# Loads of the values' matrices put into one line with those of q and k, in a top-k attention with an MLP behind it

## The chip, the cores and the metric

The kernel runs on one core of one Trainium2 chip. The metric is the device time of a run in microseconds (us). Before the change the median of three runs is 1463.46 us (1463.31 to 1465.66).

## What is computed

Per batch (8) and head (8), with 576 queries and keys of 64 elements, float32:

```python
scores = scale * np.matmul(q, k.transpose(0, 1, 3, 2))
kth = np.partition(scores, -top_k, axis=-1)[..., -top_k:-top_k + 1]   # top_k = 32
scores = np.where(scores >= kth, scores, -1000000000.0)
attn = np.exp(scores - np.max(scores, axis=-1, keepdims=True))
attn = attn / (np.sum(attn, axis=-1, keepdims=True) + 1e-09)
attn_out = np.matmul(attn, v)
x = attn_out.transpose(0, 2, 1, 3).reshape(B * S, H * D)              # 4608 x 512
h = x @ w_in                                                          # 512 x 2048
out = np.maximum(0.01 * h, h) @ w_out                                 # 2048 x 512
```

## The kernel before

**Pairs and units.** Two heads make a pair, so there are 32 pairs, four a batch. The attention is cut into 144 units, 18 a batch: a whole unit is 128 query rows of one pair, a left unit the 64 remaining rows of two pairs. In even batches the 16 whole units come first and the 2 left units last; in odd batches the left units come first. So an odd batch begins with two left units that between them touch all four of its pairs: units 18 and 19 (pairs 4 to 7), 54 and 55 (pairs 12 to 15), 90 and 91 (20 to 23), 126 and 127 (28 to 31). An even batch begins with one whole unit of each pair (36 to 39 for pairs 8 to 11).

**Steps.** The loop over s (L629 on) runs one step a unit, and an order written out by hand spreads the units in flight over the engines; each engine runs its own instructions in that order. In step s:

- VectorE picks the 32 largest scores of unit s (`top_k`, L292 to L309: eight MAX8 and six MATCH_REPLACE8 a unit), and takes the reciprocals of unit s-2 (L330);
- GpSimd masks unit s-1 (L317, L318), ScalarE takes its exponents (L321) and normalizes unit s-2 (L333);
- `transpose` (L335) turns the weights of unit s-2: ScalarE splits them into 16-bit halves (L342), SyncE writes the two halves to DRAM (L343, tile `apart`), and, once both have landed, reads them back through a transposing DMA (L347, tile `wT`). Units 14, 15, 23 and 31 are transposed on TensorE instead (L357);
- at the end of step s, from unit 14 on, TensorE multiplies the weights of two units with the values (L386 whole, L398 left, tile `vt`). Line 513, `values_at`, says when: for unit n at the end of step (n | 1) + 3, one step earlier for units 14 and 15, 22 and 23, 30 and 31. Units 54 and 55 are therefore due at the end of step 58. ScalarE copies the result to `x` (L410);
- from step 20 on, TensorE then computes the scores of units s+2 and s+3 in even steps (L228), and ScalarE copies them out (L235);
- the MLP of finished chunks of tokens (L455 and L467, with w_in and w_out) fills TensorE between these in small portions, with a budget per portion that is set so that the work is done when the next chunk is ready.

**Kept scores.** TensorE is free in the first steps, so the scores of 12 units are computed then and written to DRAM (`keep_scores`, L285). They are those of units a, a+1, a+8 and a+9 for each a of `KEPT` (L521), and come back in a fetch of 576 KB (`fetch_scores`, L290), three steps ahead of their unit.

**SyncE.** All DMAs are issued by SyncE, in its order; one that has to wait holds back those behind it. In a step the order is: halves, transposing DMA, then one of a fetch or one waiting load of q or k (L669 to L672), later an output (L477), and at the step's end what `load_more` (L567) starts. Queries and keys go into `waiting` (L162) and leave it one transfer a step. Value matrices (320 KB a pair, five buffers) do not: `load_v` (L177) issues their load at once, at the end of step last + 4, where last is the last unit of the pair that frees the buffer. At the turn to an odd batch that makes two loads at the end of each of two steps (20 and 21, 56 and 57, 92 and 93, 128 and 129, where three are left for the last); at the turn to an even batch it makes one at the end of each of four steps (36 to 39 and so on).

Of the kernel before, what the change touches and what calls it, by code (L numbers as in the profile page):

```python
# [20 lines left out]
def kernel(  # L21
# [13 lines left out]
    nc = tc.nc  # L35
    NPAIR, P, S = qT.shape
# [20 lines left out]
    LOADED, LOADED_V = 5, 5  # L57
# [102 lines left out]
    qk_of, v_of = {}, {}  # L160

    def load_qk(pi, at_once=True):  # L162
        if pi % (LOADED + 3) < LOADED:
            qt = loads.tile([P, S], F32, name="qt")
            kt = loads.tile([P, S], F32, name="kt")
        else:
            raw = raws.tile([P, WCH, 4], U16, name="raw").rearrange("p n w -> p (n w)").bitcast(F32)
            qt, kt = raw[:, 0:S], raw[:, S:2 * S]
        waiting.extend([(qt, qT[pi]), (kt, kT[pi])])
        qk_of[pi] = qt, kt  # L170
        if at_once:
            while waiting:
                nc.sync.dma_start(*waiting.pop(0))

    waiting = []

    def load_v(pi):  # L177
        v_of[pi] = loads.tile([P, NKC, 2, D], F32, name="vt", bufs=LOADED_V)
        nc.sync.dma_start(v_of[pi], vk[pi])

    class Unit:

# [71 lines left out]
    def load_early(us):  # L254

        raw = raws.tile([P, WCH, 4], U16, name="raw").rearrange("p n w -> p (n w)").bitcast(F32)
        at = 0
        for pi in sorted({u.pairs[0] for u in us}):
            kt = raw[:, at:at + S]
            nc.sync.dma_start(kt, kT[pi])  # L260
            at += S
            for u in us:
                if u.pairs[0] == pi:
                    early_of[u] = raw[:, at:at + P], kt
                    nc.sync.dma_start(early_of[u][0], qT[pi][:, u.q0:u.q0 + P])
                    at += P
# [61 lines left out]
    def reciprocals(u):  # L328
        u.rz = small.tile([P, 2], F32, name="rz")
        nc.vector.reciprocal(u.rz, u.ze)  # L330
# [175 lines left out]
    LAG = 3  # L506
# [6 lines left out]
    def values_at(n):  # L513

        if n < UNHURRIED:
            return (n | 1) + LAG + 1, MIDDLE
        return (n | 1) + LAG - ((n | 1) in HURRIED), END

    steps = units

    KEPT = (24, 40, 56)  # L521
    EARLY_SCORES = {0: 4, 1: 2, 2: 1, 3: 2, 4: 1, 5: 2}

    def unit(n):
# [26 lines left out]

    with tc.manual_schedule():
        last = {p: n for n, u in enumerate(steps) for p in u.pairs}

        to_keep = [[steps[n] for n in (a, a + 1, a + 8, a + 9)] for a in KEPT]
        early_units = {u for us in to_keep for u in us}
        to_load, to_keep = list(to_keep), [u for us in to_keep for u in us]
        assert all(len(u.pairs) == 1 for u in to_keep)

        def score_early(count):  # L560

            for _ in range(min(count, len(to_keep))):
                keep_scores(to_keep.pop(0))
                if len(to_keep) % 4 == 0 and to_load:
                    load_early(to_load.pop(0))

        def load_more(s):  # L567

            for of, load, n, lag in ((v_of, load_v, LOADED_V, LAG + 1), (qk_of, load_qk, LOADED + 3, 8)):
                if of is qk_of and to_keep:  # L570
                    while len(of) < LOADED:
                        load(len(of))
                    continue
                while len(of) < NPAIR and (len(of) < n or last[len(of) - n] + lag <= s):
                    if of is v_of or len(of) < n:
                        load(len(of))
                    else:
                        if not waiting:
                            load(len(of), at_once=False)
                        break  # L580


        for n in range(3):
            load_weights(n)
        jobs = [round_weights(*job) for job in ROUNDED] if AS_WORDS else [iter(())] * len(ROUNDED)
        for n in range(len(jobs) + 1):
            if n == len(jobs) - 1:
                first = first_scores(steps[0])
                next(first, None)
            for job in jobs[max(n - 1, 0):n + 1][::-1]:  # L590
                next(job, None)
            if n == len(jobs) - 1:
                next(first, None)
                load_v(0)
                load_v(1)
            elif n == len(jobs):
                for _ in first_scores(steps[1]):
                    pass
            if n:
                load_weights(n + 2)  # L600
            if n >= len(jobs) - 2:
                load_early(to_load.pop(0))
            if 0 <= n - len(jobs) + HP + 1 < HP:
                load_qk(n - len(jobs) + HP + 1)

        def weights_of(u):
            reciprocals(u)
            normalize(u, 0)
            normalize(u, 1)

        def values(*place):
            due = [u for n, u in enumerate(steps) if values_at(n) == place]
            if not due:
                return ()
            po = ps_sc.tile([P, 2, 512], F32, name="wide", bufs=2)
            if len(due[0].pairs) == 1:
                weigh_whole(due, po, FULL + [NKC - 1] if place[1] == MIDDLE else
                            [QUARTERS] + FULL if place[0] < HURRY else FULL + [QUARTERS])
                return [(due[0], po[:, :, 0:P])]
            for n, u in enumerate(due):  # L620
                weigh_left(u, po[:, :, n * LEFT:(n + 1) * LEFT])
            return [(u, po[:, :, n * LEFT:(n + 1) * LEFT]) for n, u in enumerate(due)]

        def keep(weighed, *place):
            for u, po in weighed:
                keep_values(u.pairs[0], po, u.b, u.q0)
            attended(*place)

        for s in range(len(steps) + LAG + 1):  # L629
            assert s < 7 or not to_keep  # L630
            cur, old, older, new = unit(s), unit(s - 1), unit(s - 2), ()
            if s % 2 == 0:
                new = [u for u in steps[s + 2:s + 4] if u]
            picks = top_k(cur) if cur else iter(())
            budget = slot_budget(s)

            def slot():
                next(picks, None)

            at_first = s < HURRY and s - 2 in HURRIED  # L640
            if at_first:
                weights_of(older)
            slot()
            if old:
                mask(old, 0)
                mask(old, 1)
            late = s < HURRY and not {s - 1, s - 2} & set(HURRIED)
            if older and not late and not at_first:
                weights_of(older)
            mlp_steps(budget)  # L650
            weighed = values(s, MIDDLE)
            at_once = s - 2 in HASTY or any(at == (s, MIDDLE) for at, _ in ready_at)
            if at_once:
                keep(weighed, s, MIDDLE)
            slot()
            if older and late:
                weights_of(older)
            if s - 2 in HASTY:
                transpose_in_haste(older)
            mlp_steps(budget)  # L660
            if old:
                exponents(old, 0)
            mlp_steps(budget)
            if older:
                keep_transposed(older) if s - 2 in HASTY else transpose(older, lambda: mlp_steps(budget))
            if not older or s - 2 in HASTY:
                mlp_steps(budget)
            if unit(s + 3) in early_units:
                fetch_scores(unit(s + 3))  # L669
            elif waiting:  # L670
                nc.sync.dma_start(*waiting.pop(0))
            slot()  # L672
            slot()
            mlp_steps(budget)
            if old:
                exponents(old, 1)
                sums(old)
            mlp_steps(budget)
            if not at_once:
                keep(weighed, s, MIDDLE)  # L680
            if new and new[0] in early_units:
                new = ()
            if new and s < HURRY:
                scores(new)
            keep(values(s, END), s, END)
            if new and s >= HURRY:
                scores(new)
            score_early(EARLY_SCORES.get(s, 0))
            budget = slot_budget(s + 1)
            mlp_steps(budget)  # L690
            load_more(s)
        mlp_steps(1e9)

# [58 lines left out]
```

## Time and profile before

| | |
|---|---|
| median of three runs | 1463.46 us |
| the profiled execution's own time | 1460.92 us |
| its span | 1458.9 us |
| granted TensorE clock over the span | 0.983 |
| TensorE, VectorE busy | 1397.0 us, 1319.8 us |
| ScalarE, GpSimd busy | 1101.0 us, 1096.4 us |
| DMA: moved, mean rate | 239.14 MB, 164 GB/s |
| SyncE: halves, transposing DMAs, loads of values | 280, 140, 32 |
| one half, one transposing DMA, one load of values, issue to landing (median) | 2.3, 4.6, 3.8 us |

A line of a timeline gives the start, the busy time, engine and line, operation, output and inputs, how many instructions were merged, and in brackets the idle time before and what ended it. PE is TensorE, PEld its weight loads, DVE VectorE, ACT ScalarE, POOL GpSimd, SPq SyncE's queue. On SPq the time is that of issuing, and the landing is told apart.

### The profile page before, as it was taken

The page shows a single profiled execution, that of the slowest core. Times are in us where ns is not written, and L with a number is a line of the kernel's source. Part 1 is how long each engine was busy: PE and PEld are TensorE (multiplying, and loading weights), DVE is VectorE, ACT ScalarE, POOL GpSimd, SP SyncE. Part 2 cuts the span into 40 slices and gives each one's busy share as a digit, 9 for nine tenths or more (in the row PEclk, how much of TensorE's full clock was granted, in tenths as well). Part 3 has the DMA queues.
Part 4 walks back from the last instruction along what each step waited for, and adds up shares of the span by engine and source line. Part 5 has one row for each costly group of instructions (what it writes and reads, how often), then busy time and mean ns, then how long its engine had stood idle before and what let it go on. Part 6 is the DMA issues. An engine that isn't in the chain of part 4 may idle for free.

```text
span 1458.9 us, 26037 instructions
## 1 busy us (share of the span) xinstructions
PE 1397.0 (96%) x8978; PEld 904.6 (62%) x8980; DVE 1319.8 (90%) x3401; ACT 1101.0 (75%) x1984; POOL 1096.4 (75%) x744
## 2 busy tenths in 40 slices
PE   7848999899989999999999999999999999999998
PEld 2324548475656666666666666666666666666674
DVE  7999999989999999999999999999999999999600
ACT  8878888577767777778787878787878787778710
POOL 3388888878887888888888888888888888788600
PEclk9968999999999999999999999999999999999999
DMA  9967544647476676667666655557555665554610
GB/s 334 338 213 228 140 119 117 185 117 185 137 192 170 179 173 161 187 167 191 169 158 165 176 145 139 166 156 177 148 161 163 171 155 130 171 138 128 154 40 14
DMA packets 394996, 239.14 MB, mean 164 GB/s; under 512 B 334576, under 2 KB 336112, under 8 KB 392944
## 3 DMA queue, kind: packets, MB, share of 16 engines
q1 hardware_dynamic: 394864, 237.48, 58.7%
q8 instruction: 70, 1.15, 0.3%
q14 instruction: 62, 0.51, 0.1%
HBM read 55.77 MB, written 99.09 MB: 106 GB/s over the span
## 4 chain that ended last, share of the span: by engine, by line
PE 74%; DVE 12%; DMA 7%; ACT 5%; issue 1%; SPq 0%; POOL 0%; DVEq 0%; ACTq 0%; POOLq 0%
PE ph L455 28%; PE pz L467 28%; PE wide L386 9%; DVE tops L304 5%; PE wide L228 4%; DVE pairs L307 4%; DMA apart<-split 3%; PE narrow L228 3%; DMA wT<-apart 3%; ACT split L342 2%; DVE pairs L299 1%; PE wide L398 1%; ACT s_sb L321 1%; ACT s_sb L333 1%; DMA raw<-in_weights_dram 1%
## 5 line engine op out<-in xcount | busy, mean ns | idle before, releaser
L317 POOL TENSOR_SCALAR pen<-s_sb,tops 128x576 f32<-128x576 f32 x288 | 637.5, 2213 | 202.0 <-DVE tops L304 130.0
L304 DVE MAX8 tops<-pairs 128x8 f32<-128x288 f32 (+1 forms) x1152 | 636.0, 591 | 0.0
L467 PE MATMUL pz<-w_out,gT 128*128 128x512 f32 x1152 | 504.7, 594 | 2.4 <-ACT scale L428 2.4
L455 PE MATMUL ph<-x,w_in 128*128 128x256 f32 x2176 | 482.6, 381 | 0.0
L307 DVE MATCH_REPLACE8 pairs<-tops,pairs 128x288 f32<-128x288 f32 (+1 forms) x864 | 460.3, 538 | 0.0
L455 PEld LDWEIGHTS ph<-x,w_in 128*128 128x128 f32 x2176 | 409.5, 190 | 77.3 <-issue 23.1
L318 POOL TENSOR_TENSOR s_sb<-s_sb,pen 128x576 f32<-128x576 f32 x288 | 406.4, 1411 | 24.1
L467 PEld LDWEIGHTS pz<-w_out,gT 128*128 128x128 f32 x1152 | 216.4, 190 | 267.0 <-issue 261.5
L342 ACT COPY split<-s_sb 128x1152 uint16<-128x1152 uint16 x280 | 309.5, 1147 | 2.3 <-DMA apart<-split 2.2
L333 ACT ACTIVATE s_sb<-s_sb,rz 128x576 f32<-128x576 f32 x288 | 207.6, 773 | 36.9 <-DVE rz L330 36.6
L321 ACT ACTIVATE s_sb<-s_sb,nbias 128x576 f32<-128x576 f32 x288 | 222.3, 772 | 5.7 <-POOL s_sb L318 5.7
L299 DVE TENSOR_TENSOR pairs<-s_sb 128x576 f32<-128x576 f32 x288 | 213.6, 780 | 9.5
L386 PE MATMUL wide<-wT,vt 128*64 128x128 f32 (+1 forms) x2560 | 160.3, 284 | 14.5 <-DMA wT<-apart 10.9
L386 PEld LDWEIGHTS wide<-wT,vt 128*64 128x64 f32 (+1 forms) x2560 | 132.4, 139 | 63.8 <-issue 41.3
L410 ACT COPY x<-wide 128x128 f32<-128x128 f32 (+1 forms) x160 | 32.2, 260 | 130.9 <-PE wide L386 114.9
L461 ACT ACTIVATE gT<-ph 128x512 f32<-128x512 f32 x136 | 80.6, 593 | 56.1 <-PE ph L455 55.8
L235 ACT COPY s_sb<-wide 128x704 f32<-128x704 f32 x130 | 98.1, 755 | 9.4 <-PE wide L228 3.6
L476 ACT COPY o_sb<-pz 128x512 f32<-128x512 f32 x36 | 21.1, 585 | 90.3 <-PE pz L467 90.3
L228 PE MATMUL wide<-kt,qt 64*64 64x352 f32 x640 | 66.3, 476 | 1.0 <-ACT s_sb L250 0.7
L235 ACT COPY s_sb<-narrow 128x448 f32<-128x448 f32 x130 | 62.9, 536 | 0.9 <-PE narrow L228 0.4
L307 DVE MATCH_VALUE_LOAD pairs<-tops,pairs 128x8 f32 x864 | 62.7, 73 | 0.0
L330 DVE RECIPROCAL rz<-ze 128x2 f32<-128x2 f32 x144 | 22.2, 154 | 39.7 <-ACT ze L326 39.3
(69 smaller groups left out, 701.8 us busy)
## 6 DMA issues: line engine op xcount, KB each, us to landing
apart<-split SPq DMA_DIRECT2D x280, 288.0 KB, 2.3
raw<-in_weights_dram SPq DMA_DIRECT2D x15, 1024.0 KB, 7.1
vt<-in_vk_dram SPq DMA_DIRECT2D x32, 320.0 KB, 3.8
out_dram<-o_sb SPq DMA_DIRECT2D x36, 256.0 KB, 3.1
kept<-gT SPq DMA_DIRECT2D x12, 576.0 KB, 3.4
s_sb<-kept SPq DMA_DIRECT2D x12, 576.0 KB, 4.8
qt<-in_qT_dram SPq DMA_DIRECT2D x20, 288.0 KB, 3.5
kt<-in_kT_dram SPq DMA_DIRECT2D x20, 288.0 KB, 3.5
```

The source lines that it names most:

```text
L228: nc.tensor.matmul(to[r0:r0 + LEFT, i, :], qt[d, q0:q0 + LEFT], kt[d, k0:k1], start=True, stop=True)
L299: nc.vector.tensor_tensor(pairs[:, :, n, :], u.both[:, :, 0:HS], u.both[:, :, HS:S], op)
L304: nc.vector.max(out=u.tops[:, i, r, :], in_=rest[i])
L307: nc.vector.match_replace(out=rest[i], in_to_replace=u.tops[:, i, r, :], in_values=rest[i], imm_value=LOWEST)
L317: nc.gpsimd.tensor_scalar(pen, u.s[i], u.tops[:, i, ROUNDS - 1, 7:8], MASKED, ALU.is_lt, ALU.mult)
L318: nc.gpsimd.tensor_tensor(u.s[i], u.s[i], pen, ALU.add)
L321: nc.scalar.activation(u.s[i], u.s[i], AF.Exp, bias=u.nbias[:, i:i + 1], scale=SCALE, accum_out=u.z[:, i:i + 1])
L333: nc.scalar.activation(u.s[i], u.s[i], AF.Copy, bias=0.0, scale=u.rz[:, i:i + 1])
L342: nc.scalar.copy(split, pairs[:, :, h])
L386: nc.tensor.matmul(po[n * D:(n + 1) * D, side, 0:P], v_of[u.pairs[0]][k, at, side, :], u.wT[k, at + side * NKC if at + 1 < NKC else at, :] ...
L455: nc.tensor.matmul(ph[:, i, 0:n], w_in[c][:, f * P:(f + 1) * P], x[c][:, 0:n], start=(c == 0), stop=(c == HP - 1),)
L467: nc.tensor.matmul(pz[0:m, 0:DMODEL], gT[:, f, r0:r0 + m], w_out[f // 4][:, f % 4, :], start=(f == 0), stop=(f == NFC - 1),)
```

## The change

A value matrix whose buffer comes free is no longer loaded at the end of the step. It goes into a line of its own, `waiting_v`, with the step in which it is first used (`due`), and the one place in the middle of a step where loads of q and k leave, after the step's transposing DMA, now serves both: values first when they are due within three steps or when nothing else waits, and a second value matrix in the same step when it is due in the next. In a step with a fetch none leaves. A matrix may enter the line as soon as the values that free its buffer have been emitted. Besides, the first group of kept units is 26, 27, 34, 35 in place of 24, 25, 32, 33.

```diff
-    def load_v(pi):
+    def load_v(pi, due=None):
         v_of[pi] = loads.tile([P, NKC, 2, D], F32, name="vt", bufs=LOADED_V)
-        nc.sync.dma_start(v_of[pi], vk[pi])
+        if due is None:
+            nc.sync.dma_start(v_of[pi], vk[pi])
+        else:
+            waiting_v.append((due, v_of[pi], vk[pi]))
+
+    def load_waiting(s):
+
+        if waiting_v and (not waiting or waiting_v[0][0] <= s + 3):
+            nc.sync.dma_start(*waiting_v.pop(0)[1:])
+            if waiting_v and waiting_v[0][0] <= s + 1:
+                nc.sync.dma_start(*waiting_v.pop(0)[1:])
+        elif waiting:
+            nc.sync.dma_start(*waiting.pop(0))
...
-    KEPT = (24, 40, 56)
+    KEPT = (26, 40, 56)
...
+        starts = {p: n for n, u in reversed(list(enumerate(steps))) for p in u.pairs}
...
-            for of, load, n, lag in ((v_of, load_v, LOADED_V, LAG + 1), (qk_of, load_qk, LOADED + 3, 8)):
...
-                while len(of) < NPAIR and (len(of) < n or last[len(of) - n] + lag <= s):
...
+            while len(v_of) < NPAIR:
+                n = len(v_of)
+                if n < LOADED_V:
+                    load_v(n)
+                elif values_at(last[n - LOADED_V])[0] <= s:
+                    load_v(n, due=values_at(starts[n])[0])
+                else:
+                    break
+            while len(qk_of) < NPAIR:
+                n = len(qk_of)
+                if n < LOADED or not to_keep and n < LOADED + 3:
+                    load_qk(n)
+                elif not to_keep and last[n - LOADED - 3] + 8 <= s and not waiting:
+                    load_qk(n, at_once=False)
+                else:
+                    break
...
             if unit(s + 3) in early_units:
                 fetch_scores(unit(s + 3))
-            elif waiting:
-                nc.sync.dma_start(*waiting.pop(0))
+            else:
+                load_waiting(s)
```

More of the change, by code (lines that the diff above doesn't have):

```diff
@@ L173, in load_qk @@
                 nc.sync.dma_start(*waiting.pop(0))
-    waiting = []
-    def load_v(pi):
+    waiting, waiting_v = [], []
+    def load_v(pi, due=None):
         v_of[pi] = loads.tile([P, NKC, 2, D], F32, name="vt", bufs=LOADED_V)
-        nc.sync.dma_start(v_of[pi], vk[pi])
+        if due is None:
[9 more added lines that the diff above has]
+            nc.sync.dma_start(*waiting.pop(0))
     class Unit:
@@ L567, in load_more @@
         def load_more(s):
-            for of, load, n, lag in ((v_of, load_v, LOADED_V, LAG + 1), (qk_of, load_qk, LOADED + 3, 8)):
[L570 to L573, printed above, removed]
-                while len(of) < NPAIR and (len(of) < n or last[len(of) - n] + lag <= s):
[L575 to L580, printed above, removed]
+            while len(v_of) < NPAIR:
[14 more added lines that the diff above has]
+                    break
         for n in range(3):
```

## Prediction

> **What bounds the kernel now.** I read the page first (busy time, then the chain that ended last), then a table of stages, then TensorE's and SyncE's timelines around the steps that first use new value matrices.
>
> ```profile
> PE 1397.0 (96%) x8978; PEld 904.6 (62%) x8980; DVE 1319.8 (90%) x3401; ACT 1101.0 (75%) x1984; POOL 1096.4 (75%) x744
> PE 74%; DVE 12%; DMA 7%; ACT 5%; issue 1%; SPq 0%; POOL 0%; DVEq 0%; ACTq 0%; POOLq 0%
> ```
>
> TensorE carries 74% of the chain. The stages show from when (columns: stretch, its length, busy us of PE, PEld, DVE, ACT, POOL with counts, granted clock, DMA share, GB/s):
>
> ```profile
> 262.00:350.00 88.00, 83.87 (x553) 54.46 (x552) 81.71 (x214) 61.70 (x118) 69.09 (x48) 0.98 0.59 157
> 350.00:440.00 90.00, 82.26 (x535) 54.14 (x535) 88.06 (x230) 63.72 (x120) 74.80 (x50) 0.96 0.63 170
> 440.00:580.00 140.00, 139.71 (x870) 93.15 (x864) 135.01 (x350) 110.46 (x201) 114.02 (x76) 1.00 0.69 173
> 580.00:700.00 120.00, 119.88 (x847) 81.97 (x844) 117.76 (x313) 94.32 (x177) 100.45 (x68) 1.00 0.66 177
> ```
>
> From 440 us on TensorE has no idle time to speak of: a stall put there moves the end by its length. Between 262 and 440 it is idle for 4.13 + 7.74 = 11.9 us. TensorE's timeline shows three of the waits (in brackets):
>
> ```profile
> 268.36 1.38 PE L398 MATMUL wide<-wT,vt 128*64 128x64 f32 x38 [2.08 <-DMA vt<-in_vk_dram]
> 286.07 3.04 PE L386 MATMUL wide<-wT,vt 128*64 128x128 f32 x38 [2.04 <-DMA wT<-apart]
> 434.85 3.67 PE L386 MATMUL wide<-wT,vt 128*64 128x128 f32 x38 [6.08 <-DMA wT<-apart]
> ```
>
> These are what the change can win: a value matrix that came late, and two transposes held up by loads of values and fetches of kept scores in front of them. The fourth (1.39 us at 397.37) has no load of values before it.
>
> What it can lose is read from step 58, where units 54 and 55 first use pairs 12 to 15. SyncE:
>
> ```profile
> 591.32 2.45 SPq L347 DMA_TRANSPOSE wT<-apart  x1
> 593.83 1.05 SPq L179 DMA_DIRECT2D vt<-in_vk_dram  x2
> 594.98 0.85 SPq L343 DMA_DIRECT2D apart<-split  x2
> 599.95 2.24 SPq L347 DMA_TRANSPOSE wT<-apart  x1
> ```
>
> and TensorE:
>
> ```profile
> 597.73 2.55 PE L398 MATMUL wide<-wT,vt 128*64 128x64 f32 x80
> 600.22 0.82 PE L228 MATMUL wide<-kt,qt 64*64 64x352 f32 x8
> ```
>
> The transpose of step 58 is issued at 599.95, *after* TensorE has begun step 58's values at 597.73. Whatever SyncE issues behind that transpose is too late for them. Before the change nothing that they need stands there.
>
> [...] So a transpose that waits for its input holds back every load behind it on SyncE. The trace agrees: SyncE's transposes waited 346.2 us in 146 waits for the halves they read, and issues behind them came after. [...] a half lands in 2.1 us with nothing ahead, in 7.5 us behind a fetch and two value matrices (issued at 264.43). [...] after the 6.08 us wait the granted clock was 0.50 until about 437.5, and the 38 matmuls took 3.67 us instead of the 2.34 of the same group at 360.89.
>
> **The change, part by part.** No arithmetic and no byte is added or removed. The listing of the changed kernel by engine gives the new order on SyncE.
>
> *Odd batches' values.* Pairs 13, 14, 15 (and 5 to 7, 21 to 23, 29 to 31) are released and queued at the end of step 56 (20, 92, 128). Before, their loads went out at the ends of steps 56 and 57. Now two go out in step 57 behind its transpose, which is SyncE's old place of the second burst, and the third in step 58 behind that step's transpose. All are needed at the end of step 58. Price, with 3.4 us from issue to landing (the 13 loads of values issued right behind a transpose took 3.1 to 4.3 by the trace, median 3.4):
> - Step 58: transpose at 599.95 + 2.24 to issue, load at 602.3, landed 605.7. TensorE needs it at the 42nd of the 80 matmuls, at 597.73 + 1.3 = 599.0. Stall 6.7 us.
> - Step 94: transpose at 927.86 + 2.25, landed 933.6; needed at 924.22 + 1.3 = 925.5. Stall 8.1 us.
> - Step 130: transpose at 1255.21, pushed to about 1256.0 because two loads now stand before it instead of one (at step 58 the second half landed 5.4 us after the second load's issue at 594.49; here that load is issued at 1250.6), + 2.6, landed 1262.0; needed at 1255.0. Stall 7.0 us.
> - Step 22: without the fetch and with two matrices ahead, the second of these is issued at about 262.7 and the halves land 5.4 us later as at step 58, at 268.1 instead of 271.9; transpose issued until 270.5, third matrix landed 273.8; needed at 266.3. Stall 7.5 us against 2.1 now: +5.4.
>
> Behind the stalled matmul on TensorE stand the rest of the values, the scores of two units and all MLP matmuls; ScalarE's x copies (L410) and score copies wait for those, then VectorE's reciprocal through ScalarE. None gives time back, since TensorE is the bound. [...] I add 1.5 us of half clock for each (1.3 lost after 434.85, 1.7 after 286.07[...]).
>
> *Relief.* The wait at 286.07 (2.04 us, then 1.7 of half clock) goes: the transpose before it comes earlier and TensorE arrives 5 us later: −3.7. At step 40 the values' burst between the two fetches is gone, so its transposes come 0.9 and 1.8 us earlier; but pair 9 now loads behind the second (428.5 + 2.4 + 3.4 = 434.3 against 434.8): −0.5, bounds −6.1 and +1.5. At step 42 pair 11 loads behind step 41's transpose and lands about 1.2 us after TensorE gets there: +1.2, bounds 0 and 1.7.
>
> *Kept units 26, 27, 34, 35 for 24, 25, 32, 33.* Four fetches of 576 KB move two steps later, past two transposes each; the scores of two units (32 matmuls, 2.1 us from 600.22 on) move from step 24 to step 22 on TensorE: zero. They come behind the stalled values, so VectorE gets unit 24's scores at about 278 instead of 274.3. Cover: VectorE's own later waits for ScalarE (2.26 and 2.69 us at 297 and 309), which TensorE's lateness caused anyway; without it up to 4 us. The second and third groups of kept units stay.
>
> *Loads of q and k.* They go out up to two steps later where a value matrix or fetch is in front. Pair 11, the tightest, is needed at step 36 and issued by step 34: zero, at most 1 us.
>
> *Sum.* Step 22 to 42: 5.4 + 1.5 − 3.7 − 0.5 + 1.2 = +3.9. Steps 58, 94, 130: 6.7 + 8.1 + 7.0 + 3 × 1.5 = +26.3. Together +30.2 on the profiled execution's 1460.92 us (span 1458.9) gives 1491.1; on the median, 2.5 higher, 1493.7. I take 1492.
>
> **Rivals.**
> - *TensorE falls behind SyncE and stalls once.* If the first stall leaves TensorE 7 us later relative to the transposes, the last matrix is in time afterwards, and only step 22 to 42 and some 1 to 2 us a batch are paid: about 1463.5 + 3.9 + 4 = 1471. For: ScalarE is 75% busy and could run ahead. Against: ScalarE already waits for TensorE at the x copies (114.9 us in 59 waits), so the others already stand as far ahead as they get.
> - *Faster: the relief wins.* If the last matrix lands before the 42nd matmul, the waits at 268, 286, 434 and 1364 (2.08 + 2.04 + 6.08 + 0.82) and 3 us of half clock go: 1463.5 − 14 = 1449.5. It decides at one place: the step's transpose would have to be issued some 7 us earlier against TensorE than at 599.95, 927.86 and 1255.21. Spoken against by all three, and by step 22.
> - *No change.* The stalls shrink to about 3 us without half clock and the relief at step 40 is full: 4 × 3 − 2.1 − 3.7 − 6.1 = 0: 1463.5. This is also the case in which the line of loads doesn't do what it says, as two still go out together. Against: two numbers would have to be off together.
>
> **How the numbers follow.** The forecast has 0.80; TensorE behind once 0.09; faster 0.07; no change 0.04. The forecast's own range, with 1.5 us either way for each of four stalls, 0 to 3 us of half clock and the bounds at step 40 and 42, is 1478 to 1503, and holds it 9 times in 10 (0.72); reaching to 1468 takes in the first rival: 1468 to 1503. A measurement here tells about 0.2% (3 us) from no change: faster 0.07, same 0.04, slower 0.89.
>
> **What would show it.** Right: TensorE waits of 6 to 9 us at the left rows' matmuls (L398, L410 in the changed kernel) for the DMA of vt, once in each of steps 22, 58, 94 and 130, with 0.50 clock after them, and the load that ends each issued directly behind a transpose; waits for transposes near 286 gone. Wrong: these waits under 3 us, or TensorE idle for other reasons after 440 us; then the place of the transpose against TensorE is not fixed as I hold it.

## The result and the profile after

The changed kernel takes 1502.1 us (median of four runs, 1500.87 to 1503.12) against 1464.56 us before (four runs beside it, 1463.31 to 1466.05): a ratio of 1.0256, with a 95% interval of 1.0238 to 1.0273. It is slower by 37.5 us, 10 us more than the forecast of 1492 us, and inside the range of 1478 to 1503 us, at its upper end. The profiled execution took 1500.87 us with a span of 1498.9 us, so 40.0 us more than the one before.

The page of the changed kernel, busy time and the chain by engine:

```profile
PE 1406.1 (94%) x8980; PEld 911.6 (61%) x8980; DVE 1322.5 (88%) x3401; ACT 1100.7 (73%) x1984; POOL 1098.3 (73%) x744
PE 72%; DVE 11%; DMA 8%; ACT 6%; issue 1%; SPq 1%; POOL 0%; DVEq 0%; ACTq 0%; POOLq 0%
```

TensorE is busy 9.1 us longer with the same matmuls (records of two are missing before), and in a span that is 40.0 us longer it is therefore idle 30.9 us more. These are the two sorts of loss that the prediction names: waiting, and matmuls at half clock. The stages from 440 us on say where (columns as in the prediction's table: stretch, length, busy us of PE, PEld, DVE, ACT and POOL with counts, granted clock, DMA share, GB/s):

```profile
440.00:580.00 140.00, 137.89 (x875) 93.58 (x872) 131.36 (x341) 105.87 (x194) 111.40 (x75) 0.99 0.66 172
580.00:700.00 120.00, 112.65 (x767) 73.43 (x766) 110.26 (x288) 87.24 (x163) 93.48 (x63) 0.97 0.62 164
```

Before, TensorE was idle for 0.12 us in the second stretch; now it is for 7.35 us, and the granted clock is 0.97 there. TensorE's waits by line and tile (sum in us, times, longest):

```profile
PE wide L410 <- DMA vt<-in_vk_dram: 31.2, 6, 7.2
PE wide L398 <- DMA vt<-in_vk_dram: 8.2, 2, 6.9
PE wide L398 <- DMA wT<-apart: 4.6, 5, 1.4
```

The changed kernel's L410 and L398 are L398 and L386 of the kernel before (left and whole rows of the values). 39.4 us go into waits for value matrices; waits for transposes at the whole rows fell from 10.9 to 4.6 us. Step 58, first on SyncE, then on TensorE:

```profile
598.09 2.42 SPq L359 DMA_TRANSPOSE wT<-apart  x1
600.56 0.57 SPq L187 DMA_DIRECT2D vt<-in_vk_dram  x1
601.18 0.42 SPq L189 DMA_DIRECT2D vt<-in_vk_dram  x1
601.65 0.95 SPq L355 DMA_DIRECT2D apart<-split  x2
607.13 2.44 SPq L359 DMA_TRANSPOSE wT<-apart  x1
609.62 0.57 SPq L187 DMA_DIRECT2D vt<-in_vk_dram  x1
```

```profile
604.47 1.75 PE L410 MATMUL wide<-wT,vt 128*64 128x64 f32 x42
613.41 2.40 PE L410 MATMUL wide<-wT,vt 128*64 128x64 f32 x38 [7.19 <-DMA vt<-in_vk_dram]
615.73 1.25 PE L240 MATMUL wide<-kt,qt 64*64 64x352 f32 x8
```

The three loads are on L187 and L189: two behind the transposing DMA of step 57, the third behind that of step 58. The group of 80 matmuls is cut at the 42nd, and the other 38 wait 7.19 us for a load that was issued at 609.62, 5.15 us after the group had begun, and landed at 613.37. The scores of two units (L240) stand behind it. The same happens in steps 22, 94 and 130, here the first and the last:

```profile
275.66 2.39 PE L410 MATMUL wide<-wT,vt 128*64 128x64 f32 x38 [7.07 <-DMA vt<-in_vk_dram]
...
1290.26 2.40 PE L410 MATMUL wide<-wT,vt 128*64 128x64 f32 x38 [7.21 <-DMA vt<-in_vk_dram]
```

In steps 22 and 94 the first of the three matrices is late too, so that TensorE waits 1.25 and 1.98 us for it before it waits for the third.

And at the turn to an even batch, steps 40 and 42:

```profile
439.00 4.03 PE L398 MATMUL wide<-wT,vt 128*64 128x128 f32 x38 [6.86 <-DMA vt<-in_vk_dram]
458.87 1.39 PE L398 MATMUL wide<-wT,vt 128*64 128x128 f32 x21 [1.32 <-DMA vt<-in_vk_dram]
```

At step 40 the wait is 0.8 us longer than before (6.08 us at 434.85), and what ends it is now a value matrix and no longer a transpose. SyncE issues that load behind the transposing DMA of step 39; first the DMA before the change, then both after it:

```profile
430.27 2.49 SPq L347 DMA_TRANSPOSE wT<-apart  x1
...
432.57 2.52 SPq L359 DMA_TRANSPOSE wT<-apart  x1
435.13 0.58 SPq L187 DMA_DIRECT2D vt<-in_vk_dram  x1
```

To set the whole against the prediction, I measured on TensorE, for each step concerned, the time from the start of the last MLP matmul ahead of the step's values to the start of the first one behind its values and scores:

| step | before, us | changed, us | difference | predicted |
|---|---|---|---|---|
| 22 and 24 | 5.40 + 8.83 | 15.32 + 2.80 | +3.9 | +3.2 |
| 30 and 32 (scores that changed places) | 2.80 + 5.43 | 4.74 + 2.80 | -0.7 | 0 |
| 40 | 12.58 | 13.71 | +1.1 | -0.5 |
| 42 | 4.97 | 6.46 | +1.5 | +1.2 |
| 58 | 5.11 | 14.31 | +9.2 | +8.2 |
| 94 | 4.89 | 15.81 | +10.9 | +9.6 |
| 130 | 5.11 | 15.26 | +10.2 | +8.5 |
| all other time | | | +3.9 | 0 |
| sum | | | +40.0 | +30.2 |

"All other time" is 0.8 us before step 22, 1.1 us between the rows and 2.0 us after step 130.

### The profile page after: what moved, and what is told of

It reads as the page before. It is cut to its first block, busy times and chain, and to the rows that moved or that the text cites. A ratio compares the mean times of both kernels' runs of the same rounds, so it can differ in the third digit from the quotient of the medians.

```text
span 1498.9 us, 26042 instructions
## 1 busy us (share of the span) xinstructions
PE 1406.1 (94%) x8980; PEld 911.6 (61%) x8980; DVE 1322.5 (88%) x3401; ACT 1100.7 (73%) x1984; POOL 1098.3 (73%) x744
## 4 chain that ended last, share of the span: by engine, by line
PE 72%; DVE 11%; DMA 8%; ACT 6%; issue 1%; SPq 1%; POOL 0%; DVEq 0%; ACTq 0%; POOLq 0%
PE ph L467 28%; PE pz L479 26%; PE wide L398 9%; PE wide L240 4%; DVE tops L316 4%; DVE pairs L319 3%; DMA wT<-apart 3%; PE narrow L240 3%; DMA apart<-split 3%; ACT split L354 2%; DMA vt<-in_vk_dram 1%; ACT s_sb L333 1%; ACT s_sb L345 1%; PE wide L410 1%; DVE pairs L311 1%
## 5 line engine op out<-in xcount | busy, mean ns | idle before, releaser
L398 PE MATMUL wide<-wT,vt 128*64 128x128 f32 (+1 forms) x2560 | 162.5, 285 | 18.4 <-DMA vt<-in_vk_dram 8.2
L398 PEld LDWEIGHTS wide<-wT,vt 128*64 128x64 f32 (+1 forms) x2560 | 134.0, 139 | 67.8 <-issue 50.1
L240 PE MATMUL wide<-kt,qt 64*64 64x352 f32 x656 | 69.8, 489 | 1.0 <-ACT s_sb L262 0.7
```

The costliest lines, as they stand in the source:

```text
L240: nc.tensor.matmul(to[r0:r0 + LEFT, i, :], qt[d, q0:q0 + LEFT], kt[d, k0:k1], start=True, stop=True)
L398: nc.tensor.matmul(po[n * D:(n + 1) * D, side, 0:P], v_of[u.pairs[0]][k, at, side, :], u.wT[k, at + side * NKC if at + 1 < NKC else at, :] ...
```

## Experiments

My theory: the loss comes from one place in the order of issue, the third value matrix behind the transposing DMA of the step that needs it, and from the half clock that follows. Rivals: the loss comes from the line as such (one transfer a step, later than before), from the kept units, or the wait costs only its length. Ten kernels were run; each time is a median, with the kernel before measured beside it on the same chip (1463.6 to 1463.9 us).

**1. The third matrix goes out with the second, in front of the transposing DMA.** An edit of the changed kernel:

```diff
-            if waiting_v and waiting_v[0][0] <= s + 1:
+            while waiting_v and waiting_v[0][0] <= s + 1:
```

> Every value matrix that is due in the next step goes out together, so the third one leaves in step 57 behind the second, not in step 58. Theory (the third matrix stands behind the transposing DMA of its own step): it is then issued about 8 us earlier and lands within 0.5 us of its use; the waits of 7.1, 7.2, 6.5 and 7.2 us go, and with them 8 us of half clock, and steps 40 and 42 stay as they are: about 1502 - 34 = 1468 us. Rival (the loss comes from the line as such, loads two steps later and their bytes beside the transposes): the bytes stay in the same steps, so at most 8 us come back: 1494 us or more.

Measured: 1466.19 us, ratio to before 1.0019 (1.0011 to 1.0027). SyncE and TensorE at step 58:

```profile
588.63 0.57 SPq L187 DMA_DIRECT2D vt<-in_vk_dram  x1
589.26 0.90 SPq L189 DMA_DIRECT2D vt<-in_vk_dram  x2
590.25 0.85 SPq L355 DMA_DIRECT2D apart<-split  x2
596.21 2.52 SPq L359 DMA_TRANSPOSE wT<-apart  x1
```

```profile
594.75 1.38 PE L410 MATMUL wide<-wT,vt 128*64 128x64 f32 x38 [0.27 <-DMA vt<-in_vk_dram]
```

One word in the code moves one load of 320 KB ahead of one transposing DMA, at four places in the program, and 36 us are back. The 7 us waits are gone at all four turns, and behind step 58 the granted clock is 1.00 (612.5 to 616.0). Half clock is left at step 40: TensorE still waits 5.59 us there, and the 38 matmuls then take 3.67 us, the same as before the change, where 0.50 was granted until 437.6. The line as such is not the cause.

**2. Every load of the line ahead of the step's transposing DMA.** An edit of the changed kernel; the line still gives one transfer a step:

```diff
+            if unit(s + 3) not in early_units:
+                load_waiting(s)
             if older:
                 keep_transposed(older) if s - 2 in HASTY else transpose(older, lambda: mlp_steps(budget))
...
-            else:
-                load_waiting(s)
```

> The same line with the same loads in the same steps, but a step's loads are issued before its halves and its transposing DMA, not behind them. Theory (place against the transposing DMA): the third matrix is issued 8 us earlier, lands before its use, and pair 9 and 11 too, so that the waits for values go at all six places; but every load of a step, q and k included, now delays that step's halves by about 1 us, which can cost up to 1 us in an even step: 1466 to 1480 us. Rival (it is the step, not the place in it): the load is still in step 58, so the time stays at about 1500 us.

Measured: 1458.12 us, ratio 0.9961 (0.9951 to 0.9972). Better than expected, and 0.4% faster than the kernel before. SyncE, then TensorE:

```profile
588.86 0.57 SPq L187 DMA_DIRECT2D vt<-in_vk_dram  x1
589.52 1.35 SPq L355 DMA_DIRECT2D apart<-split  x2
594.15 2.61 SPq L359 DMA_TRANSPOSE wT<-apart  x1
```

```profile
592.77 2.55 PE L410 MATMUL wide<-wT,vt 128*64 128x64 f32 x80
```

The third load is now issued ahead of the step's halves and no longer behind its transposing DMA, 5.3 us sooner than that DMA goes out. The group of 80 runs in one piece. TensorE waits for no value matrix anywhere. Spreading the loads costs nothing; the side of the transposing DMA on which each leaves decides.

**3. The later kept units alone.** The kernel before with one edit:

```diff
-    KEPT = (24, 40, 56)
+    KEPT = (26, 40, 56)
```

> The kernel before with the first group of kept units two later and nothing else. Theory: at the first turn the fetch no longer stands among the loads of values, so the wait for values (2.1 us), the wait for the transpose (2.0 us) and its half clock (1.7 us) go, the rest stays: 1464.5 - 5.8 = about 1459 us. Rival (moving the fetches and two units' scores is neutral, because they meet the same queue two steps later): 1463 to 1466 us.

Measured: 1458.42 us, ratio 0.9969 (0.9961 to 0.9978), as the theory had it. TensorE in steps 22, 24 and 40:

```profile
267.01 2.55 PE L398 MATMUL wide<-wT,vt 128*64 128x64 f32 x80
...
285.53 2.35 PE L386 MATMUL wide<-wT,vt 128*64 128x128 f32 x40
...
429.60 4.31 PE L386 MATMUL wide<-wT,vt 128*64 128x128 f32 x38 [6.56 <-DMA wT<-apart]
```

Both waits near 268 and 286 are gone: the kept units are the part of the change that gains, 5.5 us in the median. (This one profiled execution took 1461.41 us, no less than the one before the change: step 40 took 1.2 us longer in it, and shorter waits stood elsewhere, 1.05 us at 1270.7 for example.) The wait of step 40 stays. Loads in the line with the kept units left at 24 were not tried. By the code, the fetches of steps 21 and 22 would take the line's turns there, and pairs 5 to 7 would leave only after the values that need them, so that the line could not do without this part.

**4. The late third matrix issued by ScalarE.** An edit of the changed kernel:

```diff
-            nc.sync.dma_start(*waiting_v.pop(0)[1:])
+            late = waiting_v[0][0] == s
+            (nc.scalar if late else nc.sync).dma_start(*waiting_v.pop(0)[1:])
```

> The changed kernel, with the one load of values that is due in its own step (four in all, steps 22, 58, 94, 130) issued by ScalarE at the same place of the step instead of by SyncE. Theory (it waits in SyncE's order behind a transposing DMA that waits for its halves): ScalarE issues it when its second split is done, some 7 us earlier, and it lands about 1 to 2 us after its first use; 5 to 6 us and most half clock come back at each of four places: about 1502 - 28 = 1474 us. Rival[...]: no change, 1500 us.

Measured: 1465.75 us, ratio 1.0012 (1.0004 to 1.0019): 8 us better than I expected, and 36 us better than the changed kernel. ScalarE's queue, ScalarE, TensorE, SyncE, step 58:

```profile
592.58 0.34 ACTq L188 DMA_DIRECT2D vt<-in_vk_dram  x1
593.20 2.19 ACT L355 COPY split<-s_sb 128x1152 uint16<-128x1152 uint16 x2
597.64 2.61 PE L411 MATMUL wide<-wT,vt 128*64 128x64 f32 x80
600.24 2.28 SPq L360 DMA_TRANSPOSE wT<-apart  x1
```

The load has the same place in the code as in the changed kernel; only the queue is another. It leaves 7.7 us before the transposing DMA behind which it stood, and nothing waits for it. The rival, that the load is late whoever issues it, is ruled out. I had put it behind the two splits on ScalarE, and that was wrong (see the end). What is left is the wait at step 40 (6.58 us), 1.23 at step 42, 2.66 at step 94 and 1.85 at step 22.

**5. Two loads a step, but none in a step with a fetch.** The kernel before with `KEPT` at 26 and, in `load_more`:

```diff
-            for of, load, n, lag in ((v_of, load_v, LOADED_V, LAG + 1), (qk_of, load_qk, LOADED + 3, 8)):
+            for k in range(2):
+                n = len(v_of)
+                if n < NPAIR and n >= LOADED_V and unit(s + 3) not in early_units:
+                    if values_at(last[n - LOADED_V])[0] <= s:
+                        load_v(n)
...
```

> The kernel before with the later kept units, and its loads of values still at the end of a step: as soon as the buffer is free, two a step at most, none in a step with a fetch. Pairs 9 and 10 then load at the end of step 36, 11 and 12 at the end of 39, so that no load of values stands between the fetches of steps 37 and 38. Theory (at step 40 the loads among the fetches hold up the transposes): most of the 6.1 to 6.6 us wait there goes with 1.4 us of half clock, on top of what the later kept units give: 1458.4 - 6 = about 1452 us. Rival (the two fetches alone make that wait, as the changed kernel hints, which has no load between them and waits 6.9 us): 1458 us.

Measured: 1458.32 us, ratio 0.9956 (0.9942 to 0.9969). The gain expected at step 40 did not come:

```profile
427.36 4.31 PE L386 MATMUL wide<-wT,vt 128*64 128x128 f32 x38 [4.41 <-DMA wT<-apart]
```

With no load of values between the two fetches TensorE still waits 4.41 us, against 6.56 us in experiment 3, which has one there and one behind the second fetch. So some 2.1 us of the wait go with these loads, the larger part does not, and the total is that of the later kept units alone.

**6. The same rule for pairs 9 and later alone, kept units as before.**

```diff
...
+                if LOADED_V <= n < NPAIR and (unit(s + 3) not in early_units or n < 9):
+                    if (values_at(last[n - LOADED_V])[0] if n >= 9 else last[n - LOADED_V] + LAG + 1) <= s:
+                        load_v(n)
...
```

> The kernel before with that rule for pairs 9 and up alone; the first turn and the kept units stay as they were. Theory: the wait at step 40 shrinks by itself: 1463.9 - 6 = about 1458 us, with the waits at 268 and 286 unchanged. Rival: 1464 us.

Measured: 1461.15 us, ratio 0.9981 (0.9973 to 0.9989), between the two expectations; the wait of step 40 is 5.76 us, and the waits of the first turn, which were to stay, are 1.61 and 0.88 us. It says little beyond experiment 5.

**7. Experiment 5 with the second group of kept units two later.**

```diff
-    KEPT = (26, 40, 56)
+    KEPT = (26, 42, 56)
```

> The kernel with loads of values at the ends of steps without a fetch, with the second group of kept units at 42 instead of 40, so that its fetches are in steps 39 and 40. Theory (two fetches in a row hold up the transposes that the next values need, wherever they are): the wait of 4.4 us goes from step 40 to step 42 and stays 3 to 5 us long: 1457 to 1460 us. Rival (TensorE is early at step 40 for lack of other work, and two steps later it is not): the wait falls under 1 us, 1453 us.

Measured: 1459.66 us, ratio 0.9975 (0.9964 to 0.9985). TensorE in steps 40 and 42:

```profile
424.44 2.34 PE L386 MATMUL wide<-wT,vt 128*64 128x128 f32 x38 [1.27 <-DMA wT<-apart]
...
443.25 4.31 PE L386 MATMUL wide<-wT,vt 128*64 128x128 f32 x38 [3.89 <-DMA wT<-apart]
```

Most of the wait moves with this group of kept units; 1.27 us stay. That fits the fetches, but does not show them to be the cause by themselves. With them moves a gap on TensorE: the scores of two kept units (2.1 us) are missing two steps before the wait, so that TensorE can come earlier. And the group's later fetches (at 498.3 and 507.4 us here) and those of the third group (553.5 and 562.6) also go out in two steps running, yet the waits for transposes behind them are 0.72 us and less. What makes the wait long at this one turn stays open.

**8. The wait filled with work, four passes.** The changed kernel, which in the four steps repeats the first of the two left units' values four times (160 matmuls whose result the proper pass overwrites; nothing is left out):

```diff
+            if place[0] in (22, 58, 94, 130):
+                for _ in range(4):
+                    weigh_left(due[0], po[:, :, 0:LEFT])
```

> The changed kernel with 80 further record entries of matmuls (the products of the first of the two left units, taken four times more than needed, 5.1 us) ahead of the late matrix's first use in steps 22, 58, 94 and 130; the output stays the same. They fill idle time of TensorE. Theory (each wait costs its length and then half clock[...]): the waits shrink to about 2 us, their ends stay, the half clock after them goes: 2 us each, 1502 - 8 = about 1494 us. Rival (the half clock costs nothing on top, the excess over my sum comes from work that is late elsewhere): 1502 us; if the added matmuls cost time of their own, more.

Measured: 1495.17 us, ratio 1.021 (1.0195 to 1.0226). The total is the one expected, but not for the reason given: waits of 2.8 to 3.4 us were left behind the added matmuls, and half clock still followed at step 58 (0.52 granted behind a wait of 2.81 us). TensorE there, and a stretch behind the wait:

```profile
611.69 1.77 PE L410 MATMUL wide<-wT,vt 128*64 128x64 f32 x38 [2.81 <-DMA vt<-in_vk_dram]
```

```profile
612.50:616.00 3.50, 3.50 (x42) 2.29 (x42) 0.00 (x0) 1.30 (x5) 3.39 (x2) 0.52 0.02 5
```

So its total settles nothing about the half clock, and two more kernels were run together.

**9. The changed kernel again.**

> The changed kernel once more, unchanged, as the yardstick for the next one on the same chip: 1502 us, waits for values of 7 to 9 us in steps 22, 58, 94 and 130, and 3 to 6 us of half clock after each.

Measured: 1500.42 us, ratio 1.0248 (1.0229 to 1.0267). Waits for value matrices at the four turns 31.3 us.

**10. Six passes in place of four.**

> As the kernel with the filled wait, with the first left unit's products taken six times more instead of four (7.6 us), so that the whole wait is filled[...]; the output stays the same. Theory (half clock after a wait costs 1.6 to 2.9 us beyond the wait, which is where my sum was short): the matmuls take as long as the wait did, no half clock follows, and the four steps are 1.3, 1.6, 2.0 and 2.6 us shorter than in the changed kernel: 1502 - 7.5 = about 1494.5 us. Rival (half clock costs nothing that is not made up within a step): the filling is 0.4 us longer than each wait, 1503 us or more.

Measured: 1496.14 us, ratio 1.0229 (1.0209 to 1.0248), 4.3 us less than the changed kernel beside it, where I expected 7.5. TensorE at step 58, and the stretch around it in experiment 10, then in experiment 9:

```profile
602.43 8.49 PE L410 MATMUL wide<-wT,vt 128*64 128x64 f32 x282
611.43 1.38 PE L410 MATMUL wide<-wT,vt 128*64 128x64 f32 x38 [0.51 <-DMA vt<-in_vk_dram]
```

```profile
585.00:620.00 35.00, 34.41 (x480) 23.67 (x481) 28.27 (x72) 20.84 (x42) 27.42 (x19) 1.00 0.51 139
```

```profile
585.00:620.00 35.00, 27.60 (x261) 15.35 (x259) 28.31 (x72) 17.79 (x38) 29.53 (x21) 0.85 0.59 161
```

The granted clock stays at 1.00, and the 38 matmuls behind the wait take 1.38 us, not 2.40. Each turn has 240 more matmuls, 7.0 us (8.39 us for 280, 1.39 for 40). Over the four turns 28.0 us of added work and 5.6 us of remaining waits stand in place of 31.3 us of waits, 2.3 us more; yet the four stages of the table's sort (steps 22, 58, 94, 130) take 55.5 us in sum, not 62.3, without the added work's 28.0 us being taken off. The difference, 6.8 + 2.3 = 9.1 us or 2.3 us a turn, is what the half clock costs on top of the wait. Not all of it reaches the total: this kernel waits more at other places (1.08 us at step 56 and 1.34 us near 1024, for example), and the single times of the two kernels overlap (1494.41 to 1500.12 against 1497.92 to 1502.27). So the price is read from the stages and their clock, not from the totals.

## Why the prediction was right, and where its size was short

**The third matrix: right in place and size.** The loads stand where the listing put them, and experiments 1, 2 and 4 take the loss away by three different routes that have one thing in common, that the load leaves before the transposing DMA. In steps 58, 94 and 130 the waits are 7.19, 8.49 and 7.21 us, 22.9 in sum, against 21.8 predicted; in step 22 8.3 us against 7.5. In steps 22 and 94 these sums contain the 1.25 and 1.98 us for the first matrix, which the prediction did not have; as the third came later in any case, they add nothing to the end of the wait. The four loads landed 3.07, 3.75, 3.21 and 3.65 us after issue (3.4 assumed).

**The half clock: the mis-sized term.** The prediction gave 1.5 us a turn. In steps 58, 94 and 130 the stages grew by 30.3 us, of which the waits explain 22.9; the other 7.4 us are 2.5 a turn. Experiment 10, which removes it, gives 2.3. The prediction took its 1.5 us from the two cases of before, in which TensorE ran matmuls at half clock for 2.8 us (after 434.85) and 3.4 us (after 286.07). In the changed kernel the granted clock was 0.50 from 609.8 to 616.6, from 944.3 to 954.6 and from 1285.7 to 1295.9, and TensorE ran matmuls for 3.2, 4.2 and 5.6 us of these; half of that, 6.5 us, is my estimate of the loss, and close to the 7.4 (the last 38 matmuls of the group take 2.40 us there, and 1.38 at the 1.00 of experiment 10). So here the loss went with the time that the half clock went on after the wait had ended, which the prediction held to be the same each time. With that term at 2.5 us the sum would have been 4 us higher.

**Relief at 286: right.** The values of step 24 run at 294.35 without a wait, and steps 22 and 24 together are at +3.9 us against +3.2. Experiment 3 shows that the relief comes from the kept units, not from the line.

**Relief at step 40: wrong, +1.1 us for -0.5.** I held that the transposes would come earlier once the values' burst between the fetches was gone, and they did: the one that TensorE waits for landed 5.0 us after TensorE had stopped (437.11 against 432.14), 6.0 before (434.81 against 428.77), so 1.1 us earlier for 1.8 forecast. What failed is pair 9. It was to land 0.5 us before the old end of the wait; its load was issued 2.56 us after the transposing DMA, landed at 438.87, 3.74 us later, and ended a wait that was 0.8 us longer. Half clock (0.50 granted from 435.7 to 442.6) makes up the rest. The value lies inside the bounds given (-6.1 and +1.5), at their dear end.

**Step 42: right** (+1.5 for +1.2; 1.32 us of wait).

**What the prediction did not have.** 3.9 us lie in no step of it: 2.0 us behind step 130, 0.8 us ahead of step 22 and 1.1 us between. Of the 2.0 us, 1.7 are waits for transposes (2.5 us in three waits, 0.8 us in one before). Single executions of the kernel before range from 1459.2 to 1467.2 us, so this may be no property of the kernel; no run here settles it. It is the largest single part of the 9.8 us by which the sum was short; the half clock of steps 58, 94 and 130 is the next, with 2.9 us.

**The rivals.** TensorE does not fall behind once: the full wait stands in all four turns, 22.9 us in the last three where 1 to 2 us each were left to it. The trace shows that SyncE did not get ahead: the transposing DMA of step 58 went out 2.7 us after TensorE had begun its values (607.13 against 604.47); in the kernel before it was 2.2 us. I put that down to ScalarE, which makes the halves and waits for TensorE itself, as the prediction had it; no run takes this apart. The relief does not win, and the stalls did not shrink. The line is not bad by itself either. With the third matrix in time but all loads behind the transposing DMA it costs 7.8 us more than the later kept units alone (1466.2 against 1458.4, experiments 1 and 3), and with every load ahead of the transposing DMA nothing (1458.1, experiment 2).

Experiments 2, 3, 5, 6 and 7 are all below the kernel before. The first three, at 1458.1 to 1458.4 us, 0.3 to 0.4% under it, are not to be told apart.

## What to carry over

When a transfer is put into a line, look at the issues that it now stands behind, not at the step in which it goes out: one that waits for its input delays everything behind it (here by some 7 us, for a load that lands within 4). Take the time at which the consumer reaches its first use from its own timeline and ask of every load that is spread out whether it lands before that; here a burst that landed in time was better than a smooth line whose last piece did not. Where TensorE is the bound, price such a wait at its length and the half clock behind it; in this kernel that was a third more (7.4 us on 22.9).

## What the runs showed of the hardware that was not expected

ScalarE's queue issued the load of experiment 4 at 592.58, before the two splits that stand ahead of it in ScalarE's order had begun (593.20). In this trace the DMA issue did not wait for ScalarE's earlier work.

Half clock also followed waits much shorter than the four of 6.5 to 7.2 us: the 2.81 us in experiment 8 (0.52 granted from 612.5 to 616.0), and 2.04 us in the kernel before at 286.07 (0.50 granted from 287.4 to 290.8), while the wait of 2.08 us at 268.36 left none (1.00 granted from 264.7 to 271.0). So the length of the wait alone did not tell whether half clock followed.

Nor did it tell how long half clock went on. In the changed kernel the waits of 7.19 us at step 58 and of 7.21 us at step 130 are all but equal, and 0.50 was granted for 6.8 us at the first (609.8 to 616.6) and for 10.2 us at the second (1285.7 to 1295.9); at step 94, with waits of 1.98 and 6.51 us, it was 10.3 us (944.3 to 954.6). In the kernel before it was 3.4 us behind the 2.04 us at 286.07. No run here was made to take apart what decides it.
